# One 128-column part of Strassen's products: a21·d1 + a22·d2 written as (a21 + a22)·d1 + a22·(d2 − d1), in three of four sequence sets and in both down projections

## The chip, the core and the metric

One core of a Trainium2 chip. The time is device microseconds (us) of one execution, the median of several runs. Five engines work side by side, each with its own instruction queue in program order: PE (matmul; PEld is its weight load), DVE (vector), ACT (scalar), POOL (here nearly only a DMA queue that can also add while it writes) and SP (only a DMA queue).

## What is computed

A block of an FNet mixer with a gate: layer norm, a real 2-D Fourier mix by dense matrices, a SwiGLU feed-forward net, and x + mix · silu(ffn). S = 2048, D = 640, F = 1536, all in fp32.

```python
xn = _layernorm(x, axis=-1)
a = jnp.einsum("bsd,ed->bse", xn, dft_hid_re)
b = jnp.einsum("bsd,ed->bse", xn, dft_hid_im)
s = jnp.einsum("ts,bse->bte", dft_seq_re, a) - jnp.einsum("ts,bse->bte", dft_seq_im, b)
g = _silu((_silu(xn @ w_gate) * (xn @ w_up)) @ w_down)
return x + s * g
```

## The kernel before

**The mix** is taken in the other order: first the sequence matrices times xn (function `seq`), then the hidden matrices (`hid`). `seq` runs four times, k = 0 to 3, called sets here: half of the output columns (j = k // 2) with the real or the imaginary matrix (ri = k % 2). Then, for each of the two halves j, `hid(j)`, `gate_up(j)` (12 blocks f of 128 hidden units, gate and up together) and `down(j)` follow one another.

**Strassen.** Each large product is one Strassen step with seven products p1 to p7 instead of eight. The left operand is cut in four: a11, a12, a21, a22 (512 moving columns each; the inner width in chunks g, four of two tiles in `seq`, two of three tiles in `down`). The right operand has 640 columns, which are five blocks of 128: four of them make the 2x2 Strassen step (256 columns each side), and the fifth block is multiplied in the plain way, beside the Strassen products whose left operand is wanted anyway. The fifth block has an upper half d1 and a lower half d2 over the inner width, and two results:

- "d1" (PSUM bank 6) = a11·d1 + a12·d2, which rides on p1 (left a11) and p2 (left a12);
- "d2" (PSUM bank 7) = a21·d1 + a22·d2. Here a22 is p4's left operand, but a21 alone is no product's left operand. So a phase "d" of its own, after p1, splits a21 and multiplies it with d1.

p5's left operand is a21 + a22. In `seq` the sum is made in place by a DMA that adds (`accumulate`, line L589 before, POOL's queue): a21 is loaded (`load`, SP's queue, L576), split for "d", a22 is added to it, and the sum is split for p5. In `down` it is a DVE add into a buffer of its own (L340).

**Split.** fp32 is multiplied as high and low parts: ACT writes the high part (L192), DVE the low part (L197, or L199 with a sign), and each tile pair takes three matmuls (L213 to L215): high·high, high·low, low·high. All split operands lie in one arena, `hl`, all raw data in another, `raw`.

**Order.** Nothing is scheduled by a tool. Class `Plan` records each piece of work with a due time, in units in which one matmul takes MM = 0.226 us; work that feeds a product is due `lead` us ahead of it (`prod`), work that empties a bank after it (`post`). At the end all is sorted by due time and written to the engines' queues in that order; `place` packs all buffers of the whole program into the two arenas by their planned lives and keeps the packing with the lowest penalty for short pauses between two tenants of one place. So a change of any buffer's life can move all other buffers. A tenant that comes too early waits for the last reader of the one before.

For sets 2 to 4 the leads are: loads 17 or 18, the split's high part 10, its low part 8 (`LEAD["S"] = (10, 8)`), right operands 14 for a sum, 13 high, 11 low. The adding DMA of a22 is due 7.5 us ahead of phase "d".

**Down's right operands** (`down_operands`) are split once and kept in DRAM: a generator makes one piece per call (sum or difference on DVE where one is needed, L527; high on ACT, low on DVE, two stores on POOL, L535). `gate_up(0)` calls it twice in each block f from 1 to 10, once after p2 (slot A) and once after the next two products (slot B). Before, 18 pieces fill blocks 1 to 9. `down` fetches them on SP's queue (L996), 14 us ahead of the product for g = 0 and 10 us for g = 1.

**In gate_up** the second bank of each block is used again soon: p7 of block f writes bank b2, DVE empties it (`combine` into `u`, L246), and p4 of the same block writes b2 again after only p1 and p5 of the next block, which are 12 matmuls.

Of the kernel before, what the change touches and what calls it, by code (L numbers as in the profile page):

```python
# [11 lines left out]
ALU = mybir.AluOpType  # L12

P = 128
# [123 lines left out]
def tile_fnet_swiglu(  # L138
# [22 lines left out]
    pl = Plan()  # L161
# [90 lines left out]
    def strassen(tag, groups, get, top, dop, result, end=False):  # L252
# [52 lines left out]
        ops = {}  # L305
# [12 lines left out]
        def phase(p, banks, left, direct=None):  # L318
            w, wk = top(p) if banks else (None, None)
            need(p, left)  # L320
            run(p, ops[p], banks, w, wk, direct)
# [2 lines left out]
            Y[g] = get(11, g)  # L324
            return operand("p1", g, Y[g])

        def a21(g):
            X[g] = get(21, g)
            return operand("d", g, X[g])

        def a12(g):
            Z[g] = get(12, g)
            return operand("p2", g, Z[g])

        def s_1(g):
            V[g] = get(22, g)
            name = pl.buf(("W", tag, g), "raw", n[g])
            W[g] = (name, 0, (name, 0))
            (xn_, xa, xk), (vn, va, vk) = X[g], V[g]
            pl.prod(12, lambda: nc.vector.tensor_tensor(  # L340
                raw(name), raw(xn_, xa, n[g]), raw(vn, va, n[g]), op=ALU.add), [xk, vk], [(name, 0)])
            return operand("p5", g, W[g])
# [13 lines left out]
        phase("p1", b2, a11, (1, 1))  # L356
        s1 = copies("s1")
        evict(s1, b2)
        phase("d", None, a21, (2, 1))
        phase("p2", b1, a12, (1, 2))  # L360
        result(11, b1, s1, ALU.subtract)
        result("d1", (dbank[1],), None, None)
        phase("p5", b3, s_1)
        n5 = copies("n5")
        evict(n5, b3)
        phase("p6", b2, s_2)
# [10 lines left out]
        w, wk = top("p4")  # L377
        need("p4", a22)
        if not end:
            run("p4", ops["p4"], None, None, None, (2, 2))  # L380
            result("d2", (dbank[2],), None, None)
            run("p4", ops["p4"], b2, w, wk)
            result(21, b2, None, None)
            return
        dw, dkeys = dop(2)

        def alone(bank, weights, keys, first, a=0, n=TC):

# [80 lines left out]
    def right(p, g, lead):  # L469


        def quad(h, c, w=256):
            k = 8 * h + 4 * g
            return (lambda a=0, n=4: xn_tiles(k + a, n, 256 * c, w)), [(xn, i, c) for i in range(k, k + 4)]

        def new(what, a, b, op):
            if (what, g) not in sums:
                name = pl.buf((what, g), "raw", 1024)
                view = lambda a=0, n=4: raw(name).rearrange("p (a b) -> p a b", b=256)[:, a:a + n]
                pl.prod(lead, lambda: nc.vector.tensor_tensor(view(), a[0](), b[0](), op=op), [*a[1], *b[1]], [(name, 0)])  # L480
                sums[what, g] = view, [(name, 0)]
            return sums[what, g]

        if p == "p1":
            return quad(0, 0)
        if p == "p2":
            return quad(1, 0)
        if p == "p3":
            return quad(1, 1)
        if p == "p5":  # L490
            return new("nt1", quad(0, 0), quad(0, 1), ALU.subtract)
        if p == "p6":
            return new("t2", quad(1, 1), sums["nt1", g], ALU.add)
        if p == "p4":
            return new("nt4", quad(1, 0), sums["t2", g], ALU.subtract)
        if p == "p7":
            a, b = quad(0, 1), quad(1, 1)
            if ("nt3", g) not in sums:
                pl.prod(lead, lambda: nc.vector.tensor_tensor(a[0](), a[0](), b[0](), op=ALU.subtract), b[1], a[1])
                sums["nt3", g] = a  # L500
            return a
        return quad(int(p[1]) - 1, 2, P)


    d_names = ("p1", "p2", "d1", "d2", "p3", "p5", "p6", "p7", "p4")
    d_dram = {(p, g): dram.tile([P, 768 if p[0] == "d" else 1536], F32, name=f"d_{p}_{g}") for g in range(2) for p in d_names}

    def down_operands():

        for g in range(2):  # L510
            name = pl.buf(("wdn", g), "raw", 6 * D)
            for h in range(2):
                f0 = 6 * h + 3 * g
                pl.prod(8, lambda name=name, f0=f0, h=h: nc.sync.dma_start(
                    raw(name, 3 * h * D, 3 * D).rearrange("p (f d) -> p f d", d=D),
                    wb[f0:f0 + 3, :, 2 * D:].rearrange("f p d -> p f d")), [], [(name, h)])

            def quad(h, c, w=256, name=name):
                return (lambda: raw(name, 3 * h * D, 3 * D).rearrange("p (f d) -> p f d", d=D)[:, :, 256 * c:256 * c + w]), (name, h, c)

            for p in d_names:
                b11, b12, b21, b22 = (quad(*q) for q in ((0, 0), (0, 1), (1, 0), (1, 1)))
                made = {"p5": (b11, b12, ALU.subtract), "p6": (b11, b22, ALU.add),
                        "p7": (b12, b22, ALU.subtract), "p4": (b21, b11, ALU.subtract)}
                if p in made:
                    a, b, op = made[p]
                    pl.prod(1, lambda a=a, b=b, op=op: nc.vector.tensor_tensor(a[0](), a[0](), b[0](), op=op),  # L527
                            [b[1], (name, 0), (name, 1)], [a[1]])
                else:
                    a = {"p1": b11, "p2": b21, "p3": b22, "d1": quad(0, 2, P), "d2": quad(1, 2, P)}[p]  # L530
                n = 768 if p[0] == "p" else 384
                dst = pl.buf(("Tp", p, g), "hl", 2 * n)
                split(0, dst, n, a[0], [a[1], (name, 0), (name, 1)], scale=-1.0 if p == "p1" else None)
                for i in range(2):
                    pl.prod(-4, lambda p=p, g=g, dst=dst, i=i, n=n: nc.gpsimd.dma_start(  # L535
                        d_dram[p, g][:, i * n:i * n + n], hl(dst, i).bitcast(F32)),
                        [(dst, "hl"[i], 0)], [("dd", p, g)], 6)
                yield
# [15 lines left out]
    def seq(k):  # L554
# [157 lines left out]
            return operand("p1", g, Y[g])  # L712

        def p5(g):
            s = operand("p5", g, R[g])
            if fresh:
                accumulate(R[g], 11, g, LEAD["p5", g][1] - 0.1)
            return s

        def d(g):  # L720
            R[g] = load(21, g, 26 if fresh else 18)
            s = operand("d", g, R[g])
            if ("d", g) not in whole:
                accumulate(R[g], 22, g, LEAD["d", g][1] - 0.1 if fresh else 7.5)
            return s

        def p2(g):
# [26 lines left out]
            run(first_two[0])  # L754
        s1 = copy("s1", b2)
        if not fresh:
            run(first_two[1])
        if not fresh:
            product_2()
        run(("p5", p5, b3, None), order=((0, 0), (0, 2), (0, 3), (0, 1)) if fresh else None)  # L760
        n5 = copy("n5", b3)
        if fresh:
            product_2()
# [9 lines left out]
            last.append(operand("p4", g, load(22, g, 17)))  # L773
            return last[-1]

        run(("p4", p4, (), (2, 2)))
        result("d2", (dbank[2],), None, None)
        run(("p4", lambda g: last[g], b2, None))
        result(21, b2, None, None)
# [330 lines left out]
```

## Time and profile before

| what | value |
|---|---|
| median of 3 runs | 994.55 us (992.47 to 995.25) |
| span of the profiled execution | 990.3 us |
| busy share in that span: PE, PEld, DVE, ACT, POOL | 99%, 81%, 72%, 50%, 11% |
| granted PE clock, mean of the span | 1.000 |
| set 1, with the start | to about 113 us |
| sets 2, 3 and 4 | about 113 to 211, to 309, to 407 us |
| gate_up(0), down(0) | about 475 to 622, 622 to 696 us |
| gate_up(1), down(1) | about 764 to 911, 911 to 986 us |

The median stands 4.2 us above the span, since a run also has time ahead of the first and behind the last instruction that the profile shows, and since runs differ. The page's busy numbers are averages over stages with different limits; the waits, told engine by engine, say which engine was ever held up and by whom. The lines themselves stand in the prediction.

### The profile page before, as it was taken

What the parts mean: (1) busy time and instruction counts of PE and PEld (TensorE: products, weight loads), DVE (VectorE), ACT (ScalarE), POOL (GpSimd) and SP (SyncE); (2) the same over time, 40 slices, a digit from 0 to 9 for tenths busy, and PEclk for the clock granted to TensorE, in tenths of its full rate; (3) what the DMA queues carried; (4) which work ended last, traced back from release to release, by engine and by line L of the source; (5) the groups of instructions that cost most, each with busy time, mean ns of one, the idle gap of its engine ahead of it and who ended that gap; (6) DMA issues with size and microseconds to landing.
All of it is one profiled execution on the core that took longest, in us unless ns stands there. A gap on an engine that the chain in (4) does not pass through costs nothing. (4 is left out here: it accounts for less than half of the span.)

```text
span 990.3 us, 11726 instructions
## 1 busy us (share of the span) xinstructions
PE 981.1 (99%) x4302; PEld 802.9 (81%) x4302; DVE 710.3 (72%) x927; ACT 497.2 (50%) x712; POOL 105.0 (11%) x175
## 2 busy tenths in 40 slices
PE   8999999999999999999999999999999999999998
PEld 4778888888888888888888888888888888887887
DVE  6999667856785686377678787777577566666686
ACT  5775554655465564434555654444334544445342
POOL 1640201010101010000111110000010100000000
PEclk9999999999999999999999999999999999999999
DMA  9995757675766586832447535679951301106673
GB/s 342 242 226 168 249 136 179 208 210 116 189 219 187 117 236 205 275 135 94 160 149 263 189 139 176 214 258 335 332 177 54 107 28 53 54 27 205 227 266 131
DMA packets 71464, 180.08 MB, mean 182 GB/s; under 512 B 6448, under 2 KB 22064, under 8 KB 71408
## 3 DMA queue, kind: packets, MB, share of 16 engines
q1 hardware_dynamic: 57072, 125.71, 38.0%
q0 software_dynamic: 14336, 53.63, 19.7%
q8 instruction: 33, 0.54, 0.2%
q14 instruction: 23, 0.19, 0.1%
HBM read 145.75 MB, written 33.57 MB: 181 GB/s over the span
## 5 line engine op out<-in xcount | busy, mean ns | idle before, releaser
L213 PE MATMUL ps<-hl 128*128 128x512 f32 x1420 | 551.9, 389 | 1.3 <-ACT raw L979 0.7
L215 PE MATMUL ps<-hl 128*128 128x512 f32 x1420 | 551.5, 388 | 1.1 <-DVE hl L197 1.0
L214 PE MATMUL ps<-hl 128*128 128x512 f32 x1420 | 551.4, 388 | 0.3 <-DVE hl L197 0.3
L192 ACT ACTIVATE hl<-raw 128x1024 fp32r<-128x1024 f32 (+6 forms) x503 | 371.9, 788 | 263.5 <-PE ps L214 63.1
L197 DVE TENSOR_TENSOR hl<-raw,hl 128x1024 fp32r<-128x1024 f32 (+5 forms) x432 | 391.2, 936 | 133.1 <-ACT hl L192 68.3
L213 PEld LDWEIGHTS ps<-hl 128*128 128x128 f32 x1420 | 266.6, 188 | 59.6 <-ACT hl L192 3.2
L215 PEld LDWEIGHTS ps<-hl 128*128 128x128 f32 x1420 | 266.6, 188 | 57.7 <-DVE hl L197 1.8
L214 PEld LDWEIGHTS ps<-hl 128*128 128x128 f32 x1420 | 266.6, 188 | 55.3 <-DVE hl L197 0.8
L241 ACT ACTIVATE raw<-ps 128x512 f32<-128x512 f32 (+1 forms) x122 | 80.3, 676 | 128.9 <-PE ps L215 111.7
L246 DVE TENSOR_TENSOR raw<-ps,raw 128x512 f32<-128x512 f32 (+1 forms) x90 | 71.5, 795 | 58.8 <-PE ps L215 57.7
L980 DVE TENSOR_TENSOR raw<-raw 128x512 f32<-128x512 f32 x24 | 16.6, 692 | 49.3 <-ACT raw L979 49.2
L893 DVE TENSOR_TENSOR raw<-raw 128x256 f32<-128x256 f32 (+1 forms) x96 | 47.7, 518 | 0.0
L199 DVE SCALAR_TENSOR_TENSOR hl<-raw,hl 128x384 fp32r<-128x384 f32 (+5 forms) x71 | 43.0, 605 | 4.9 <-PE ps L214 2.5
L589 POOL DMA_DIRECT2D raw<-in_cs x36 | 31.8, 953 | 132.4 <-DVE raw L592 88.4
L592 DVE TENSOR_TENSOR raw<-raw 128x1024 f32<-128x1024 f32 x28 | 34.1, 1217 | 8.7 <-DMA raw<-in_cs 8.7
L1042 POOL DMA_DIRECT2D out<-raw x10 | 6.7, 672 | 303.1 <-ACT hl L192 187.5
L693 POOL DMA_DIRECT2D p_dram<-raw x24 | 17.2, 758 | 201.8 <-DVE raw L246 151.8
L958 ACT ACTIVATE raw<-raw 128x512 f32<-128x512 f32 x24 | 15.2, 632 | 22.8 <-DVE raw L246 22.8
L846 DVE TENSOR_TENSOR raw<-raw 128x1024 f32<-128x1024 f32 (+1 forms) x24 | 23.9, 1040 | 1.7 <-DMA raw<-in_xt 1.7
L818 POOL DMA_DIRECT2D y_dram<-raw x20 | 10.9, 546 | 132.5 <-ACT raw L241 132.5
L979 ACT ACTIVATE raw<-ps 128x512 f32<-128x512 f32 x24 | 14.3, 595 | 19.2 <-PE ps L215 17.4
L535 POOL DMA_DIRECT2D d_p<-hl x28 | 15.1, 541 | 80.9 <-ACT hl L192 66.9
(48 smaller groups left out, 196.5 us busy)
## 6 DMA issues: line engine op xcount, KB each, us to landing
raw<-in_cs SPq DMA_DIRECT2D x79, 512.0 KB, 6.3
hl<-d_p SPq DMA_DIRECT2D x56, 384.0 KB, 4.3
raw<-in_cs POOLq DMA_DIRECT2D x36, 512.0 KB, 8.4
raw<-in_wb SPq DMA_DIRECT2D x24, 640.0 KB, 3.9
d_p<-hl POOLq DMA_DIRECT2D x28, 384.0 KB, 3.0
raw<-p_dram SPq DMA_DIRECT2D x8, 1280.0 KB, 9.3
p_dram<-raw POOLq DMA_DIRECT2D x16, 512.0 KB, 5.7
raw<-in_hd SPq DMA_DIRECT2D x20, 320.0 KB, 8.4
```

The lines of the kernel that those rows point to most:

```text
L192: nc.scalar.activation(like(hl(dst, 0, a, n)), src(), AF.Copy, scale=1.0 if scale is None else scale)
L197: nc.vector.tensor_tensor(lo, src(), hi, op=ALU.subtract)
L199: nc.vector.scalar_tensor_tensor(lo, src(), scale, hi, op0=ALU.mult, op1=ALU.subtract)
L213: nc.tensor.matmul(o, w(0), m(0), start=first, stop=False, skip_group_check=True)
L214: nc.tensor.matmul(o, w(0), m(1), start=False, stop=False, skip_group_check=True)
L215: nc.tensor.matmul(o, w(1), m(0), start=False, stop=True, skip_group_check=True)
L241: pl.post(lambda: nc.scalar.activation(wide(raw(dst, a, n)), pair(b), AF.Copy), pkeys(b), [(dst, a)], after)
L246: pl.post(lambda: nc.vector.tensor_tensor(wide(raw(dst, a, n)), pair(b), wide(raw(other)), op=op), [*pkeys(b), (other, 0)], [(dst, a)], after)
L589: pl.prod(lead, lambda: nc.gpsimd.dma_start(wide(raw(name)), source(q, g), accum_op=ALU.add), [], [(name, 0), (name, 1)], 8)
L592: pl.prod(lead, lambda: nc.vector.tensor_tensor(raw(dst), raw(dst), raw(src), op=ALU.add), [(src, 0)], [(dst, 0)])
L846: pl.prod(46 - 6 * q - 2 * i - half, lambda i=i, op=op, part=part, rows=rows, nb=nb: nc.vector.tensor_tensor(part(), part(), raw(rows, i * ...
L893: pl.prod(lead, lambda o=o, a=a, b=b, op=op: nc.vector.tensor_tensor(o(), a(), b(), op=op), [(w, 0)], [(c, lead)])
```

## The change

In sets 2 to 4 and in both `down` calls the result "d2" is now computed as (a21 + a22)·d1 + a22·(d2 − d1). The first product rides on p5, whose left operand is that sum, the second on p4. Phase "d" and its split of a21 go away there. A third right operand "d3" = d2 − d1 is new: in `seq` a DVE difference `nt5` (made once, kept to the end of set 4) and a split in each of the three sets; in `down` one more piece per g from the generator, which now makes 20 pieces and fills blocks 1 to 10. Set 1 keeps the old way. In sets 2 to 4 the load of a21 is now due 26 us and the adding DMA of a22 18 us ahead of p5.

```diff
@@ strassen (down)
-        def a21(g):
-            X[g] = get(21, g)
-            return operand("d", g, X[g])
...
         def s_1(g):
-            V[g] = get(22, g)
+            X[g], V[g] = get(21, g), get(22, g)
...
-        phase("d", None, a21, (2, 1))
         phase("p2", b1, a12, (1, 2))
...
-        phase("p5", b3, s_1)
+        phase("p5", b3, s_1, (2, 1))
...
-            run("p4", ops["p4"], None, None, None, (2, 2))
+            run("p4", ops["p4"], None, None, None, (2, 3))
...
-        dw, dkeys = dop(2)
+        dw, dkeys = dop(3)
@@ right (seq)
+        if p == "d3":
+            return new("nt5", quad(1, 2, P), quad(0, 2, P), ALU.subtract, P)
@@ down_operands
-    d_names = ("p1", "p2", "d1", "d2", "p3", "p5", "p6", "p7", "p4")
+    d_names = ("p1", "p2", "d1", "d2", "d3", "p3", "p5", "p6", "p7", "p4")
...
+                        "d3": (quad(1, 2, P), quad(0, 2, P), ALU.subtract)}
@@ seq
         def p5(g):
+            if not fresh:
+                R[g] = load(21, g, 26)
+                accumulate(R[g], 22, g, 18)
             s = operand("p5", g, R[g])
...
         if not fresh:
-            run(first_two[1])
-        if not fresh:
             product_2()
-        run(("p5", p5, b3, None), order=((0, 0), (0, 2), (0, 3), (0, 1)) if fresh else None)
+        run(("p5", p5, b3, None if fresh else (2, 1)), order=((0, 0), (0, 2), (0, 3), (0, 1)) if fresh else None)
...
-        run(("p4", p4, (), (2, 2)))
+        run(("p4", p4, (), (2, 2 if fresh else 3)))
```

How the instructions now stand. PE's list has the same 4309 rows in the same order with the same shapes; only which operands they read and which bank they write differs. DVE, all forms counted: 12 low splits of 128x1024 and 4 of 128x1536 go; 6 of 128x512, 2 of 128x384, 2 differences of 128x512 and 2 of 128x384 come. ACT: 12 high splits of 128x1024 and 4 of 128x1536 go, 6 of 128x512 and 2 of 128x384 come. POOL has 4 more stores, SP 8 more fetches.

POOL's queue in set 2 (`raw<-in_cs` is an adding DMA, `p_dram<-raw` a store of a result). Before:

```order
54 L693 DMA p_dram_74<-raw_66 128x2x512
55 L589 DMA raw_66<-in_cs 128x1024 x7
56 L693 DMA p_dram_74<-raw_66 128x2x512
57 L693 DMA p_dram_74<-raw_66 128x512
58 L589 DMA raw_66<-in_cs 128x1024
```

And now:

```order
54 L691 DMA p_dram_74<-raw_66 128x2x512
55 L587 DMA raw_66<-in_cs 128x1024 x5
56 L691 DMA p_dram_74<-raw_66 128x2x512
57 L691 DMA p_dram_74<-raw_66 128x512
58 L587 DMA raw_66<-in_cs 128x1024 x3
```

The first four of the eight adding DMAs feed p5, in both versions ahead of everything else in this stretch; the two stores of p2's results now stand ahead of three of the four that feed p7.

DVE in gate_up(0), block 10 (`L527`, now `L525`, is a generator's difference, `L246` empties a bank, `hl<-raw,hl` is a low split). Before, with no piece in this block:

```order
438 L197 TENSOR_TENSOR hl<-raw,hl 128x384
439 L246 TENSOR_TENSOR raw<-ps,raw 128x512
440 L197 TENSOR_TENSOR hl<-raw,hl 128x256
441 L199 SCALAR_TENSOR_TENSOR hl<-raw,hl 128x384
442 L246 TENSOR_TENSOR raw<-ps,raw 128x512
443 L966 TENSOR_TENSOR raw<-raw 128x512
444 L893 TENSOR_TENSOR raw<-raw 128x256
445 L246 TENSOR_TENSOR raw<-ps,raw 128x512
446 L197 TENSOR_TENSOR hl<-raw,hl 128x384
```

And now, with pieces p7 and p4 of g = 1:

```order
456 L197 TENSOR_TENSOR hl<-raw,hl 128x384
457 L525 TENSOR_TENSOR raw<-raw 128x3x256
458 L246 TENSOR_TENSOR raw<-ps,raw 128x512
459 L197 TENSOR_TENSOR hl<-raw,hl 128x256
460 L199 SCALAR_TENSOR_TENSOR hl<-raw,hl 128x384
461 L197 TENSOR_TENSOR hl<-raw,hl 128x768
462 L246 TENSOR_TENSOR raw<-ps,raw 128x512
463 L965 TENSOR_TENSOR raw<-raw 128x512
464 L525 TENSOR_TENSOR raw<-raw 128x3x256
465 L892 TENSOR_TENSOR raw<-raw 128x256
466 L246 TENSOR_TENSOR raw<-ps,raw 128x512
467 L197 TENSOR_TENSOR hl<-raw,hl 128x384
468 L197 TENSOR_TENSOR hl<-raw,hl 128x768
```

The last L246 in each of the two lists is the one that p4 waits for; one more difference now stands right ahead of it. Blocks whose two slots both hold a piece with such a 768-wide difference were 4, 8 and 9; now they are 4, 5, 9 and 10.

SP's fetches for down(0)'s p4, as they now stand (before, only the rows of d_p4 were there):

```order
48 L995 DMA hl_65<-d_p4_0_84 128x768 x2
49 L995 DMA hl_65<-d_d3_0_79 128x384 x2
50 L995 DMA hl_65<-d_p4_1_94 128x768 x2
51 L995 DMA hl_65<-d_d3_1_89 128x384 x2
```

They stand ahead of the loads for the last results of that product.

`place` also gives nearly all buffers other places, from the first set on. From its table of places and due times: before, no split part in gate_up(0) came onto a buffer whose last reader was a store to DRAM due less than 6 us earlier. Now six do:

| split part (engine) | due | comes onto, whose store is due |
|---|---|---|
| p2, g 0, low (DVE) | 485.0 | p1, g 0, low, 482.9 |
| p3, g 0, high (ACT) | 507.4 | d3, g 0, high, 507.3 |
| p4, g 0, low (DVE) | 533.8 | p7, g 0, high, 531.7 |
| p2, g 1, low (DVE) | 546.0 | p1, g 1, low, 543.9 |
| p6, g 1, low (DVE) | 582.6 | p5, g 1, high, 580.5 |
| down(0)'s p1, g 0, high (ACT) | 598.0 | p4, g 1, high, 596.8 |

More of the change, by code (lines that the diff above doesn't have):

```diff
@@ L474, in quad, with new @@
             return (lambda a=0, n=4: xn_tiles(k + a, n, 256 * c, w)), [(xn, i, c) for i in range(k, k + 4)]
-        def new(what, a, b, op):
+        def new(what, a, b, op, w=256):
             if (what, g) not in sums:
-                name = pl.buf((what, g), "raw", 1024)
-                view = lambda a=0, n=4: raw(name).rearrange("p (a b) -> p a b", b=256)[:, a:a + n]
+                name = pl.buf((what, g), "raw", 4 * w)
+                view = lambda a=0, n=4: raw(name).rearrange("p (a b) -> p a b", b=w)[:, a:a + n]
                 pl.prod(lead, lambda: nc.vector.tensor_tensor(view(), a[0](), b[0](), op=op), [*a[1], *b[1]], [(name, 0)])
@@ L523, in down_operands @@
                 made = {"p5": (b11, b12, ALU.subtract), "p6": (b11, b22, ALU.add),
-                        "p7": (b12, b22, ALU.subtract), "p4": (b21, b11, ALU.subtract)}
+                        "p7": (b12, b22, ALU.subtract), "p4": (b21, b11, ALU.subtract),
+                        "d3": (quad(1, 2, P), quad(0, 2, P), ALU.subtract)}
                 if p in made:
@@ L720, in d @@
         def d(g):
-            R[g] = load(21, g, 26 if fresh else 18)
+            R[g] = load(21, g, 26)
             s = operand("d", g, R[g])
             if ("d", g) not in whole:
-                accumulate(R[g], 22, g, LEAD["d", g][1] - 0.1 if fresh else 7.5)
+                accumulate(R[g], 22, g, LEAD["d", g][1] - 0.1)
             return s
```

## The prediction

> **What bounds the kernel now.** I read the page's first part, then the busy time by stretches, then the waits of PE and PEld alone, then the groups with their shapes.
>
> ```profile
> PE 981.1 (99%) x4302; PEld 802.9 (81%) x4302; DVE 710.3 (72%) x927; ACT 497.2 (50%) x712; POOL 105.0 (11%) x175
> PEclk9999999999999999999999999999999999999999
> ```
>
> PE is busy for 99% of the span at the full granted clock. A busy PE need not be a PE at its peak, so the pace has to be checked. The stretches (start:end, length, then each engine's busy us and instructions, granted clock, DMA share, GB/s):
>
> ```profile
> 100.00:900.00 800.00, 799.94 (x3529) 661.87 (x3528) 562.45 (x739) 396.10 (x595) 71.37 (x111) 1.00 0.54 171
> 900.00:985.00 85.00, 84.31 (x385) 70.06 (x384) 59.46 (x47) 34.56 (x32) 2.72 (x4) 1.00 0.64 222
> 113.30:211.20 97.90, 97.90 (x433) 81.09 (x433) 68.44 (x61) 52.36 (x56) 11.01 (x14) 1.00 0.67 189
> 622.50:696.00 73.50, 73.50 (x326) 60.83 (x326) 56.38 (x44) 31.58 (x29) 3.28 (x5) 1.00 0.82 273
> ```
>
> In 800 us PE ran 3529 matmuls, one each 800/3529 = 0.2267 us. Set 2 (third row) has 7 products x 8 tiles x 2 banks x 3 matmuls and 4 x 8 x 3 for the fifth block, 432 in all: 432 x 0.2267 = 97.9 us, its whole length. So PE runs at one pace without a gap, whatever operand it reads. Who ever held it up after set 1's start, in the waits of 62 to 985 us (us in total, times, longest):
>
> ```profile
> PEld ps L213 <- ACT raw L979: 1.1, 1, 1.1
> PEld ps L213 <- DVE raw L246: 0.9, 3, 0.5
> PE ps L213 <- ACT raw L979: 0.7, 1, 0.7
> ```
>
> The first and the third are one event, down(1)'s start behind the last silu that empties a bank; the second are three short waits in gate_up(0). That is 2.0 us in 923. Anything that merely frees DVE or ACT elsewhere can give back no more than that.
>
> **The change part by part.** *PE.* Its list has the same rows before and now: the 24 matmuls of phase "d" in each set, and the 18 in each `down`, ride on p5 instead. At one pace for all operands this costs and saves 0.0 us. *DVE and ACT*, by their groups (busy us, mean ns of one):
>
> ```profile
> L197 DVE TENSOR_TENSOR hl<-raw,hl 128x1024 fp32r<-128x1024 f32 x185 | 218.8, 1219 | 68.2 <-ACT hl L192 29.1 <-issue 21.2 <-PE ps L215 10.7
> L192 ACT ACTIVATE hl<-raw 128x1024 fp32r<-128x1024 f32 x191 | 191.6, 1051 | 107.5 <-PE ps L215 30.5 <-PE ps L214 25.9 <-DVE raw L860 14.5
> L197 DVE TENSOR_TENSOR hl<-raw,hl 128x1536 fp32r<-128x1536 f32 x32 | 55.7, 1754 | 13.9 <-ACT hl L192 8.4 <-PE ps L215 3.4 <-PE ps L214 1.4
> L192 ACT ACTIVATE hl<-raw 128x1536 fp32r<-128x1536 f32 x32 | 46.8, 1484 | 35.9 <-DVE raw L290 15.8 <-PE ps L214 14.6 <-PE ps L215 5.2
> L197 DVE TENSOR_TENSOR hl<-raw,hl 128x512 fp32r<-128x512 f32 x60 | 41.1, 686 | 26.7 <-issue 8.2 <-ACT hl L192 7.7 <-PE ps L214 6.3
> L192 ACT ACTIVATE hl<-raw 128x384 fp32r<-128x384 f32 x76 | 38.4, 513 | 0.0
> L192 ACT ACTIVATE hl<-raw 128x512 fp32r<-128x512 f32 x61 | 37.6, 625 | 27.4 <-PE ps L215 17.4 <-PE ps L214 7.9 <-DVE raw L846 2.1
> L197 DVE TENSOR_TENSOR hl<-raw,hl 128x384 fp32r<-128x384 f32 x52 | 28.5, 551 | 0.8 <-ACT hl L192 0.6 <-PE ps L215 0.2
> L980 DVE TENSOR_TENSOR raw<-raw 128x512 f32<-128x512 f32 x24 | 16.6, 692 | 49.3 <-ACT raw L979 49.2
> ```
>
> DVE loses 12 x 1.219 + 4 x 1.754 = 21.6 us and gets 6 x 0.686 + 2 x 0.692 + 2 x 0.551 and two 384-wide differences at about the same 0.551, 7.7 us: 13.9 us less. ACT loses 12 x 1.051 + 4 x 1.484 = 18.6 and gets 6 x 0.625 + 2 x 0.513 = 4.8: 13.8 us less. In sets and `down` neither was waited for, so this saves 0.0 us of the span. What hides the added work: `nt5` and d3's split are due 14, 13 and 11 us ahead of p4, beside p7 (48 x 0.2267 = 10.9 us); without that cover it would be 0.69 + 0.63 + 0.69 = 2.0 us at the start of each set's p4. The d3 fetches in `down` have 10 to 14 us.
>
> *p5's operand in sets 2 to 4.* The adding DMA had the whole of p2 as cover; now it has 18 us, and the split waits for it. The adding line and the load it adds to (duration min/median/max in ns; landing in us):
>
> ```profile
> L589 POOL DMA_DIRECT2D raw<-in_cs x36: 851/871/1874, 21.6 to 353.4; - x36
> DMA to landing us min/median/max: 5.3/8.4/16.4
> DMA to landing us min/median/max: 3.1/6.3/12.1
> ```
>
> The second row is of the adds, the third of SP's loads (L576). A load has 26 − 18 = 8 us, 6.3 at the median. The add lands at 8.4, then 1.05 on ACT and 1.22 on DVE: 18 − 8.4 − 2.3 = 7.3 us to spare. At the longest landing, 18 − 16.4 − 2.3 = −0.7: PE would wait 0.7 us once a set, 2.1 us in all. Queued behind a waiting split on ACT is the copy of p1's banks, and p6, which writes these next, comes only after p2 and p5. The 16.4 us stand in set 1, where four adds are issued together; here they come one per chunk, 18 matmuls or 4.1 us apart. I take 0.0, bounds 0.0 and +2.1. The Trainium skill, "SBUF — State Buffer" (section "SBUF: two separate sides"), says that DVE in a two-port mode can keep POOL from writing a DMA's descriptors, and gives about 620 ns alone against 3100 overlapped. Here the longest issue is 1.0 us above the median, and 2.5 us more would still leave 4.8 of the 7.3, so the sum by that rule is the same, but it makes the upper end likelier.
>
> *gate_up(0).* This is where PE does wait. The timeline of block 9's end:
>
> ```profile
> 597.12 0.95 DVE L527 TENSOR_TENSOR raw<-raw 128x768 f32<-128x768 f32 x1
> 597.99 0.42 DVE L893 TENSOR_TENSOR raw<-raw 128x256 f32<-128x256 f32 x1
> 598.11 1.15 ACT L192 ACTIVATE hl<-raw 128x768 fp32r<-128x768 f32 x2 [2.81 <-DVE raw L527]
> 598.33 0.68 DVE L246 TENSOR_TENSOR raw<-ps,raw 128x512 f32<-128x512 f32 x1
> 599.06 0.19 PEld L213 LDWEIGHTS ps<-hl 128*128 128x128 f32 x1 [0.48 <-DVE raw L246]
> ```
>
> Slot B's difference, 0.95 us, runs ahead of the L246 that empties p4's bank, and PE waits 0.48 us. The three waits of 0.9 us match the three blocks with a difference in both slots (4, 8, 9): 0.48 in block 9, which follows another such block, and 0.4 for the other two, 0.2 each. Now there are four such blocks, in two runs of two: 2 x (0.2 + 0.5) = 1.4 us, so **+0.5 us**. Bounds: −0.9 (all gone) and four times 0.5 less 0.9, +1.1.
>
> *The six new buffer waits.* A generator's store:
>
> ```profile
> DMA to landing us min/median/max: 2.1/3.0/7.1
> ```
>
> With 3.0 us to land, the four on DVE with 2.1 us between the due times wait 0.9 each, the two on ACT 2.9 and 1.8: 8.3 us at most if PE got all of it. I take 0.0: on DVE the low part stands behind the L246 that PE waits for (order lists), and delays only weights of the next block. On ACT the wait takes the place of one that is there: the 2.81 us in the row above is ACT idle in slot B for the difference, and the new tenant p3 needs none.
>
> **The sum**: 990.3 + 0.0 (PE) + 0.0 (DVE, ACT relief) + 0.0 (adds) + 0.5 (gate_up) + 0.0 (buffers) = 990.8 us of span. The runs' median is 994.55 − 990.3 = 4.2 us above the span, so 995.0 us.
>
> **The rivals.** A measurement of this kernel tells about 0.3%, 3 us, from no change: faster is under 991.6, slower over 997.5.
>
> *Buffer waits reach PE (slower).* Place: gate_up(0), which has the highest DVE load of the long stages beside its bank hand-offs:
>
> ```profile
> 475.00:622.50 147.50, 147.44 (x650) 121.49 (x649) 112.25 (x208) 82.49 (x162) 22.16 (x41) 1.00 0.53 186
> ```
>
> 112 of 147.5 us, 76%. If the four DVE waits are passed on, 3.6 us: 994.55 + 3.6 = 998.2; with the two on ACT 1002.9. It decides from a landing of 2.9 us on, if nothing hides it. For it: stores landed as late as 7.1. Against it: the order and the 24% of DVE left. A stall costs its own length as long as the clock holds, as after the 1.1 us wait at down(1)'s start (granted 1.00 in 900 to 985). The Trainium skill, "TensorE: Matmul & The Clock Gate" (section "Part 1: The HAM clock gate"), puts the half-rate state after an idle window of about 3.4 us; a wait of that length, which no row after 62 us shows, would cost more by it.
>
> *The add lands late (slower).* 2.1 us at the longest landing seen, 996.7; from 16.7 us on, or if POOL comes to its issue 1.0 us late on top (3 x 1.7 = 5.1 us, 999.7), it is slower.
>
> *The relief ends the waits.* All 2.0 us go: 992.6. Against it: down(1)'s wait is for a silu that the change leaves where it is.
>
> *Set 1 gets better places (faster).* Its instructions are unchanged, its buffers move, and it is the one stage where PE waits for splits, in 9 to 65 us:
>
> ```profile
> PEld ps L213 <- ACT hl L192: 3.2, 4, 1.3
> PEld ps L215 <- DVE hl L197: 1.8, 2, 0.9
> PEld ps L215 <- DVE hl L199: 0.9, 3, 0.6
> PEld ps L214 <- DVE hl L197: 0.8, 1, 0.8
> ```
>
> 6.7 us; half of it gives 991.2. Against it: ACT's own idle time there is for DMAs and DVE, not for PE to leave a buffer.
>
> *It does not do what it says.* The words could mean a product less; PE's equal lists exclude it.
>
> **How the numbers follow.** Forecast 995.0: 0.60. Buffer waits: 0.12, slower. Late adds: 0.10, half within 0.3%, half slower. Relief: 0.08, within. Set 1: 0.10, faster. So faster 0.10, within 0.3% 0.60 + 0.05 + 0.08 = 0.73, slower 0.12 + 0.05 = 0.17. The range goes from 992.0 (the lowest run before, 992.47, and the relief's 992.6) to 998.5 (the DVE waits' 998.2). The likeliest case alone is 993.0 to 996.5, about the spread of the runs before.
>
> **What would show it.** Right: PE again one matmul each 0.2267 us from 100 to 900, no PE wait behind an adding DMA, four instead of three waits of PEld for the line that empties banks (L246), 1.4 us in all; DVE near 696 and ACT near 483 us busy. Wrong: a PE wait for L192 or L197 at p5 of sets 2 to 4 (late adds); waits for L192 in 500 to 625 us (buffers); a first 62 us that is shorter or longer by over 1 us; or a pace of PE other than 0.2267, which would upset the ground of the whole sum.

## The result, and the profile after

| | before | after |
|---|---|---|
| median of 18 runs each, on the same chip | 992.57 us (990.85 to 995.52) | 998.53 us (995.10 to 1001.18) |
| ratio of the runs, 95% interval | | 1.0054 [1.0044, 1.0065] |
| span of the profiled execution | 990.3 us | 998.5 us |
| mean granted PE clock of that span | 1.000 | 0.996 |

The change makes the kernel slower by about 5.4 us (0.0054 x 992.57; the two medians lie 6.0 us apart). The forecast was 995.0 us, no change; its range ended at 998.5, and the median stands at that end. The rival "buffer waits reach PE" is what happened, mainly at another of its six places than those its first price was for.

First the page of the kernel after: busy time, and the granted clock.

```profile
PE 985.3 (99%) x4302; PEld 804.2 (81%) x4302; DVE 694.8 (70%) x923; ACT 482.5 (48%) x704; POOL 107.4 (11%) x179
...
PEclk9999999999999999999999999999999999999999
```

DVE has 15.5 us less work than before and ACT 14.7 less; POOL has 2.4 more. PE's busy time, with the same instructions, is 4.2 us longer. At slices of 25 us the clock row shows nothing. The groups of the splits (busy us, mean ns of one) are as costed, 12 of each kind fewer at an unchanged price:

```profile
L197 DVE TENSOR_TENSOR hl<-raw,hl 128x1024 fp32r<-128x1024 f32 x173 | 205.1, 1219 | 74.6 <-ACT hl L192 55.1 <-PE ps L215 9.6 <-PE ps L214 5.1
L192 ACT ACTIVATE hl<-raw 128x1024 fp32r<-128x1024 f32 x179 | 180.3, 1052 | 96.3 <-DVE raw L590 28.4 <-DMA raw<-in_cs 19.5 <-PE ps L214 15.4
```

Who held up PE, then PEld, from 62 to 985 us (us in total, times, longest):

```profile
PE ps L213 <- ACT raw L241: 3.9, 2, 3.5
PE ps L213 <- ACT raw L978: 0.7, 1, 0.7
PE ps L213 <- DVE raw L246: 0.2, 1, 0.2
...
PEld ps L213 <- ACT raw L241: 4.8, 2, 3.9
PEld ps L213 <- DVE raw L246: 1.7, 4, 0.6
PEld ps L213 <- ACT raw L978: 1.1, 1, 1.1
PEld ps L214 <- DVE hl L197: 0.5, 1, 0.5
```

New is L241, the copy on ACT of a bank. It made PE wait 3.5 us at one time (the other time, 0.5 us, is in set 3). The stretches (start:end, length, each engine's busy us and instructions, granted clock, DMA share, GB/s), first two of those that were shown of before, then the 22 us around that wait:

```profile
113.30:211.20 97.90, 97.90 (x434) 81.06 (x433) 66.06 (x61) 49.71 (x54) 11.13 (x14) 1.00 0.63 177
...
475.00:622.50 147.50, 143.72 (x629) 117.55 (x629) 112.84 (x213) 81.98 (x164) 24.31 (x45) 1.00 0.48 171
...
612.00:618.00 6.00, 5.91 (x26) 4.59 (x25) 4.01 (x8) 3.07 (x6) 1.08 (x2) 1.00 0.89 261
618.00:622.00 4.00, 0.64 (x3) 0.19 (x1) 0.39 (x1) 1.91 (x2) 0.00 (x0) 0.91 1.01 401
622.00:628.00 6.00, 5.88 (x14) 4.63 (x15) 3.54 (x4) 2.17 (x3) 0.00 (x0) 0.50 1.02 390
628.00:634.00 6.00, 6.00 (x28) 4.94 (x27) 3.48 (x5) 2.62 (x3) 0.00 (x0) 0.99 0.32 94
```

Set 2 takes the same 97.9 us. In gate_up(0), PE stands still for nearly 4 us from 618, and then works for 6 us at a granted clock of 0.50: it counts as busy, with 14 matmuls where 26 are usual. By these rows the clock is at 0.50 for 6.8 us in all, from about 621.3 to 628.1 us: 0.7 us of that lie in the row of 0.91, and 0.1 in the row of 0.99. Now the place itself: ACT's timeline (start, length, then what it waited for before), the PE's, and the one store on POOL that was issued at 613.1 us.

```profile
615.77 0.52 ACT L192 ACTIVATE hl<-raw 128x384 fp32r<-128x384 f32 x1
620.09 1.48 ACT L192 ACTIVATE hl<-raw 128x1536 fp32r<-128x1536 f32 x1 [3.81 <-DMA d_p<-hl]
621.48 0.58 ACT L241 ACTIVATE raw<-ps 128x512 f32<-128x512 f32 x1
```

```profile
618.25 0.39 PE L215 MATMUL ps<-hl 128*128 128x512 f32 x1
622.12 0.80 PE L213 MATMUL ps<-hl 128*128 128x512 f32 x1 [3.48 <-ACT raw L241]
622.71 0.63 PE L214 MATMUL ps<-hl 128*128 128x512 f32 x1
623.13 0.63 PE L215 MATMUL ps<-hl 128*128 128x512 f32 x1
...
627.83 0.52 PE L214 MATMUL ps<-hl 128*128 128x512 f32 x1
628.19 0.40 PE L215 MATMUL ps<-hl 128*128 128x512 f32 x1
```

```profile
L533 POOL DMA_DIRECT2D d_p<-hl x1: 540/540/540, 613.1 to 613.1; - x1
...
who waited for it (us, times):
  ACT hl L192: 3.8, 1
...
DMA to landing us min/median/max: 6.9/6.9/6.9
```

The store is the generator's last but one, p4 g 1 high. It took 6.9 us to land. Its buffer's next tenant is the high part of down(0)'s p1 g 0 (plan: due 598.0, which the profile's clock reaches some 18 us later), a split for the next stage, not urgent. But ACT works in order: it stood idle 3.81 us for that buffer, made the 1.48 us split, and only then the copy L241 of `u2`, which empties the bank that p7 of block 11, the last block, writes. From 618.25 to 622.12 is 3.87 us between two matmuls, 3.64 more than one pace. The 14 matmuls from 622.12 to 628.19 take 6.07 us instead of 3.17, another 2.90.

One more of the six new waits shows in this trace, the first of the table of due times: DVE's low split of p2 g 0, behind the store of p1 g 0 low that was issued at 498.4 us and took 5.9 us to land.

```profile
504.38 0.96 DVE L197 TENSOR_TENSOR hl<-raw,hl 128x768 fp32r<-128x768 f32 x1 [3.55 <-issue]
```

DVE stood idle 3.55 us. PE noticed little of it: DVE then worked with only two short pauses (0.63 and 0.32 us) up to an L246 that ended at 514.08, and the matmul that needed that bank came 0.46 us late. In copy_first and filler, described below, DVE waits 3.1 and 3.2 us here and PEld 0.2 at that bank; in holdlast8 neither waits.

**The whole difference of the two spans**, by when the same matmul starts in both traces: start and set 1 −0.35 us, set 3's p3 +1.18, the gate waits of gate_up(0) ahead of block 11, less those of before, +0.48 (0.46 of it the one at 514 us), block 11 +6.88 (3.64 + 2.90, and one gate wait of 0.36), and from there to the end 0.0; sum +8.2 = 998.5 − 990.3. Set 3's part is a load that waits for the buffer of a stored "d1" result and lands late; the traces of the other kernels with these sets show 0 to 0.4 us there.

The runs' 5.4 us are less than this pair's 8.2. Of the 18 runs after, 14 have a mean clock of 0.996 to 0.998 and 4 one of 1.000, so the half pace seems not to come every time; and set 1 varies on its own, which the last experiment takes up.

### The profile page after: what moved, and what is told of

It reads as the page before. It is cut to its first block, busy times and chain, and to the rows that moved or that the text cites. A ratio compares the mean times of both kernels' runs of the same rounds, so it can differ in the third digit from the quotient of the medians.

```text
span 998.5 us, 11703 instructions
## 1 busy us (share of the span) xinstructions
PE 985.3 (99%) x4302; PEld 804.2 (81%) x4302; DVE 694.8 (70%) x923; ACT 482.5 (48%) x704; POOL 107.4 (11%) x179
## 4 chain that ended last, share of the span: by engine, by line
PE 87%; DMA 5%; DVE 2%; issue 2%; ACT 2%; POOL 1%; SPq 0%; DVEq 0%; POOLq 0%; ACTq 0%
PE ps L213 29%; PE ps L215 29%; PE ps L214 29%; DMA raw<-in_cs 2%; DMA raw<-in_x 2%; DVE hl L197 1%; ACT hl L192 1%; DMA p_dram<-raw 1%; DMA d_p<-hl 1%; ACT raw L451 0%; DVE raw L590 0%; ACT raw L241 0%; POOL d_p L533 0%; DVE raw L246 0%; DVE raw L475 0%
## 5 line engine op out<-in xcount | busy, mean ns | idle before, releaser
L192 ACT ACTIVATE hl<-raw 128x1024 fp32r<-128x1024 f32 (+6 forms) x495 | 358.0, 773 | 230.6 <-DVE raw L892 54.6
L197 DVE TENSOR_TENSOR hl<-raw,hl 128x1024 fp32r<-128x1024 f32 (+5 forms) x424 | 374.7, 915 | 131.1 <-ACT hl L192 99.8
L241 ACT ACTIVATE raw<-ps 128x512 f32<-128x512 f32 (+1 forms) x122 | 80.1, 675 | 171.2 <-PE ps L215 146.5
L246 DVE TENSOR_TENSOR raw<-ps,raw 128x512 f32<-128x512 f32 (+1 forms) x90 | 71.5, 795 | 71.0 <-PE ps L215 70.5
L1036 ACT ACTIVATE raw<-raw 128x1024 f32<-128x1024 f32 x6 | 6.4, 1062 | 38.6 <-DVE raw L246 32.8
```

The source lines that it names most:

```text
L192: nc.scalar.activation(like(hl(dst, 0, a, n)), src(), AF.Copy, scale=1.0 if scale is None else scale)
L197: nc.vector.tensor_tensor(lo, src(), hi, op=ALU.subtract)
L241: pl.post(lambda: nc.scalar.activation(wide(raw(dst, a, n)), pair(b), AF.Copy), pkeys(b), [(dst, a)], after)
L246: pl.post(lambda: nc.vector.tensor_tensor(wide(raw(dst, a, n)), pair(b), wide(raw(other)), op=op), [*pkeys(b), (other, 0)], [(dst, a)], after)
```

## The experiments

Theory A: the store's landing behind one ACT wait, and the half pace after it, are nearly the whole loss; the arithmetic costs nothing. The rivals: the traffic and operands of the new arithmetic cost it; or any stall costs only its own length. Each ratio is to runs of before taken in the same rounds on the same chip, so it is not always the quotient of two medians shown here. Since set 1 varies between executions, the last column gives, from the traces, the time from one matmul behind set 1's p2 (at about 77 us) to the same one in down(0) (at about 653 us), less that of before, 576.27 us.

| kernel | median us | ratio to before, 95% | behind set 1, us |
|---|---|---|---|
| after | 998.53 | 1.0054 [1.0044, 1.0065] | +8.5 |
| copy_first | 995.05 | 1.0018 [1.0002, 1.0033] | +2.5 |
| holdlast8 | 992.97 | 0.9999 [0.9986, 1.0012] | +0.2 |
| filler | 997.43 | 1.0032 [1.0017, 1.0046] | +4.6 |
| bef_shift | 1001.53 | 1.0079 [1.0056, 1.0102] | +8.2 |
| seq_only | 992.62 | 1.0007 [0.9993, 1.0020] | +0.3 |
| down_only | 1000.55 | 1.0085 [1.0065, 1.0105] | +7.1 |
| alternate | 994.13 | 0.9999 [0.9982, 1.0016] | −0.5 |
| bef_alt | 993.79 | 0.9995 [0.9979, 1.0010] | −0.5 |
| alt_ln | 992.56 | 1.0005 [0.9995, 1.0014] | −0.5 |
| bef_ln | 993.39 | 1.0008 [0.9998, 1.0018] | 0.0 |

**copy_first: the copy goes ahead of the waiting split.** Buffers unchanged; only the place of one instruction in ACT's list.

```diff
     where.update(pl.place({"hl": HL_KB * 256, "raw": RAW_KB * 256}))
+    names = [o[3] for o in pl.ops]
+    late = next(i for i, n in enumerate(names) if (("S", ("down", 0), "p1", 0), "h") in n)
+    copy = next(i for i, n in enumerate(names) if ("u2", 0, NF - 1) in n)
...
+    pl.ops.insert(copy, pl.ops.pop(late))
```

> The changed kernel with two neighbours on ACT's list exchanged: in block 11 of gate_up(0) the copy of p6's bank (u2) now stands ahead of down(0)'s first split, which waits for a store to land on its buffer. All buffers keep their places, so the wait itself stays. Theory A (the time is lost because the bank copy stands behind that waiting split, so that PE waits 3.9 us in block 11 and then runs about 6 us at half pace): the wait of PE for L241 and the 427 ns matmuls vanish, a wait of at most 1 us appears at down(0)'s p1; of the 8.2 us between the two profiles 1.3 + 0 to 1 us remain; ratio to before 0.999 to 1.003. Rival B (the time is lost to the late adds at p5, to more traffic or to the layout as a whole): ratio stays at 1.005.

No wait for L241 is left and no matmul at half pace. ACT still waits for the store, and passes a part on. Who held up PE there, and DVE's rows:

```profile
PE ps L213 <- DVE raw L246: 1.4, 1, 1.4
```

```profile
619.85 1.76 DVE L197 TENSOR_TENSOR hl<-raw,hl 128x1536 fp32r<-128x1536 f32 x1 [4.07 <-ACT hl L192]
621.53 1.28 DVE L246 TENSOR_TENSOR raw<-ps,raw 128x512 f32<-128x512 f32 x2
```

Behind its gate wait, block 11 loses 1.75 us instead of 6.54 (3.64 + 2.90). The order on ACT is thus the way from the store to PE; swapping it takes away the long wait and the half pace. What stays goes the same way on another queue: the low part of the late split waits for ACT on DVE, and the L246 that empties a bank stands behind it. That wait of 1.4 us was expected at down(0)'s p1 and at 1 us at most.

**holdlast8: that one store's buffer is kept longer.** `place` is told that the store of p4 g 1 needs 8 us instead of 6, so that it deals other tenants; by its table none of the six pairs is left.

```diff
-                        [(dst, "hl"[i], 0)], [("dd", p, g)], 6)
+                        [(dst, "hl"[i], 0)], [("dd", p, g)], 8 if (p, g) == ("p4", 1) else 6)
```

> The changed kernel with one planner number changed: the two stores of the last right-operand piece (p4, g = 1) are taken to hold their buffer 8 us instead of 6. The planner then gives other places, and by its table no split part of gate_up(0) or of down(0)'s start comes onto a buffer whose store is due less than 6 us earlier; all seven or so instructions per piece are the same. Theory A: PE's wait for L241 in block 11 and the half pace are gone, the waits for L246 in blocks 4, 5, 9 and 10 stay (about 1.4 us), the wait of set 3's p3 stays (about 1 us): ratio 0.999 to 1.003. Rival B (the arithmetic of the change costs the time): 1.005.

The loss is gone: 0.9999, +0.2 us behind set 1. The stores landed no sooner. Line L533 in 594 to 640 us, and the gate waits:

```profile
DMA to landing us min/median/max: 2.6/2.7/7.4
```

```profile
PEld ps L213 <- DVE raw L246: 1.3, 4, 0.5
```

A store of 7.4 us costs nothing where nobody needs its buffer. The four gate waits that the forecast counted, behind blocks 4, 5, 9 and 10, are all there; set 3's wait, which was expected to stay, is not. Since this kernel removes all six pairs, it is copy_first that tells which one cost the most.

**filler: PE kept busy through the wait.** 18 bf16 matmuls into a bank that is free, ahead of block 11's p7; the wait stays. They are work that the kernel before and after does not have.

```diff
+                if j == 0 and f == NF - 1 and p == "p7":
+                    pl.post(lambda: busy(ps[:, 0], 18), [], [("ps", 0)])
                 product(todo, reads)
```

> The changed kernel with 18 bf16 matmuls into the unused bank 0 ahead of block 11's p7 in gate_up(0), where PE stood still for 3.9 us; they take 18 x 0.213 = 3.8 us at full pace, so they fill the wait and compute nothing that is used. If the half pace after the wait comes from PE having stood still: PE runs 0.227 us a matmul behind them and about 2.9 us of the 8.2 are won back, ratio about 1.002 to 1.003 against 1.005. If the slow matmuls have another cause (operands arriving late, a bank in use): they stay, ratio 1.005 or more.

Granted clock in the stretches before, in and after the wait:

```profile
618.00:622.00 4.00, 3.93 (x19) 2.31 (x18) 1.03 (x2) 1.97 (x2) 0.00 (x0) 1.00 1.01 356
622.00:626.00 4.00, 4.00 (x19) 2.76 (x18) 1.74 (x2) 1.56 (x2) 0.00 (x0) 1.00 1.03 401
```

The clock is 1.00 throughout, and the matmuls behind the wait run at full pace while the DMA engines are as busy (1.03) as in the kernel after (1.02). What is saved behind set 1 is 8.5 − 4.6 = 3.9 us: the half pace (2.9) and most of set 3's 1.2. One thing weakens this trace: its set 1 was late, so PE reached the place at 619.60 us and not at 618.25, while the copy came at about the same time. Without the 18 matmuls PE would have stood still for only some 2.3 us (an estimate from these times), and no trace here shows half pace after so short a wait. The runs speak more clearly: all nine have a mean clock of 0.999 or 1.000, against 0.996 to 0.998 in 14 of the 18 of the kernel after. So the 2.9 us go with PE's standing still, and not with the traffic; the next experiment shows half pace at little traffic.

**bef_shift: the same conflict in the kernel before.** Old arithmetic; the generator starts one block later, so that it ends in block 10. The line stands twice, for slots A and B.

```diff
-            if j == 0 and f and f != NF - 1:
+            if j == 0 and f > 1 and f != NF - 1:
                 next(spare, None)
```

> The kernel before, with its arithmetic, but the generator of right operands begun one block later, so that its 18 pieces fill blocks 2 to 10 instead of 1 to 9. No instruction is added or taken away. By the planner's table down(0)'s first split (ACT, due 598.0) then comes onto the buffer of the last piece, whose store is due at 596.8, as in the changed kernel. Theory A: PE waits 3 to 4 us for L241 in block 11 and then runs at half pace, 4 to 7 us, ratio 1.004 to 1.007. Rival B (the change's arithmetic, adds or fetches cost the time): ratio 1.000.

PE's wait in 500 to 640 us, and the clock behind it:

```profile
PE ps L213 <- ACT raw L241: 5.7, 1, 5.7
```

```profile
624.00:630.00 6.00, 4.55 (x11) 3.59 (x12) 2.60 (x3) 3.40 (x4) 0.00 (x0) 0.50 0.11 18
```

The loss of the change, +8.2 us behind set 1, without one instruction of the change; in other parts, though: 5.8 us of standing still and 2.3 at half pace. The wait and the ratio (1.0079) are above what was expected (3 to 4 us, 1.004 to 1.007). The DMA engines were busy for 0.11 of the time in this row, so traffic is not what slows these matmuls.

**seq_only and down_only: each half of the change alone.** seq_only keeps `strassen` and `down_operands` as before; down_only keeps `right` and `seq` as before. Against the kernel after, the lines that matter:

```diff
@@ seq_only
-    d_names = ("p1", "p2", "d1", "d2", "d3", "p3", "p5", "p6", "p7", "p4")
+    d_names = ("p1", "p2", "d1", "d2", "p3", "p5", "p6", "p7", "p4")
@@ down_only
-        if p == "d3":
-            return new("nt5", quad(1, 2, P), quad(0, 2, P), ALU.subtract, P)
...
-            if not fresh:
-                R[g] = load(21, g, 26)
-                accumulate(R[g], 22, g, 18)
```

> The change in sets 2 to 4 alone; both `down` and the generator's list of pieces are as before. Theory A (the store of p4 g 1 high meets its buffer's next tenant at 598.0 and holds the u2 copy that p7 of block 11 waits for; nothing else costs more than 1 or 2 us): the list has no piece d3, the buffers are dealt as before and the conflict is not there, so no PE wait for L241 and no matmuls at 427 ns; three gate waits for L246, 0.9 us; what may stay is set 3's wait of 1.2 us; ratio to before 0.999 to 1.002. Rival B (the arithmetic itself costs: the p5 sum over the inner width, its adding DMA and the longer p5 operand in the sets): about two thirds of the loss is here, ratio 1.003 to 1.004, with PE waits for L192 or L197 at p5 of sets 2 to 4.

> The change in both `down` alone, with d3 in the generator's list; the sets are as before. Theory A: the list of pieces is that of the changed kernel, p4 g 1 high falls on the buffer that down(0)'s p1 g 0 high is due on at 598.0, so a PE wait for L241 of 3 to 6 us in block 11 and some 12 matmuls at 427 ns behind it come back; set 3's wait does not; ratio 1.003 to 1.007. Rival B: two of six differences' worth of the loss at most, in the two `down` themselves and not in gate_up(0); ratio 1.000 to 1.002.

seq_only, PEld from 62 to 985 us:

```profile
PEld ps L213 <- DVE raw L246: 1.1, 3, 0.5
PEld ps L213 <- ACT raw L982: 1.1, 1, 1.1
```

down_only, PE in 500 to 640 us, and the two stores of p4 g 1 (line L531):

```profile
PE ps L213 <- ACT raw L241: 3.9, 1, 3.9
```

```profile
DMA to landing us min/median/max: 7.2/7.3/7.4
```

Three sets of new arithmetic cost nothing: from matmul to matmul, sets 2 to 4 together take 0.05 us more than before, and 0.2 us lie in gate_up(0). All of the loss comes with the generator's longer list. In the runs down_only loses more than the whole change (1.0085 against 1.0054, over the 1.007 expected), in its trace less (+7.1 against +8.5, of which 1.2 are set 3's); this difference was not followed up.

**alternate and bef_alt: the list in another order.** The kernel after, and the kernel before, with pieces that have a difference and pieces that have none taking turns.

```diff
@@ alternate
-    d_names = ("p1", "p2", "d1", "d2", "d3", "p3", "p5", "p6", "p7", "p4")
+    d_names = ("p1", "p5", "p2", "p6", "d1", "p7", "d2", "p4", "p3", "d3")
@@ bef_alt
-    d_names = ("p1", "p2", "d1", "d2", "p3", "p5", "p6", "p7", "p4")
+    d_names = ("p1", "p5", "p2", "p6", "d1", "p7", "d2", "p4", "p3")
```

> The changed kernel with one line of it in another order: the generator's list of pieces alternates those with a difference and those without (p1 p5 p2 p6 d1 p7 d2 p4 p3 d3). Theory A: no new tenant falls due within the 3 us of a store's landing, so no wait for L241 in block 11 and no half pace (6.9 us less than the changed kernel's profile); no block has a 768-wide difference in both slots, so the four gate waits for L246 (1.7 us in the changed kernel, 0.9 before) go too; set 3's wait of 1.2 us may stay. Ratio to before 0.998 to 1.001. Rival B: the work is that of the changed kernel to the last instruction, so the ratio stays at 1.004 to 1.006.

> The kernel before with the list of its nine pieces alternated in the same way (p1 p5 p2 p6 d1 p7 d2 p4 p3), the arithmetic untouched. It asks whether the alternating order is worth something by itself. Theory A: the three gate waits of 0.9 us go, no buffer conflict comes, ratio 0.998 to 1.000, and between this kernel and the changed kernel with the alternated list there is at most set 3's 1.2 us, 0.001. Rival B: as before, 1.000, and the changed kernel with the alternated list stands 0.004 to 0.006 above it.

alternate, PEld from 62 to 985 us:

```profile
PEld ps L213 <- ACT hl L192: 1.2, 1, 1.2
PEld ps L213 <- ACT raw L978: 1.1, 1, 1.1
PEld ps L215 <- DVE hl L197: 0.9, 1, 0.9
```

No wait for L246 or L241 is left; the first and third rows are the end of a late set 1. Both kernels take the same 575.73 us behind set 1. The change as arithmetic is therefore worth 0.0 us, and between the two orders of the list lie 9.1 us in the traces of the new kernel (1.2 of them in set 3, where no other trace shows more than 0.4), 0.5 in those of the old.

**alt_ln and bef_ln: why runs of one kernel differ by 3 us.** The 18 runs of before fall into ten from 990.85 to 992.58 us and eight from 994.55 to 995.52, with none between. In the first ten traces the same matmul behind set 1's p2 starts at 75.4 to 77.3 us in five and at 79.4 to 80.0 in the other five. POOL's small layer norm operations for the third pair of chunks, and the DVE row beside them: first copy_first (early), then holdlast8 (late).

```profile
49.37 3.28 DVE L197 TENSOR_TENSOR hl<-raw,hl 128x1024 fp32r<-128x1024 f32 x4
...
48.67 0.19 POOL L441 TENSOR_SCALAR sm<-mv 128x2 f32<-128x2 f32 x1
...
49.39 1.24 POOL L444 TENSOR_SCALAR sm<-sm 128x2 f32<-128x2 f32 x1
...
51.31 0.26 POOL L446 TENSOR_TENSOR sm<-sm,rowst 128x2 f32<-128x2 f32 x1
```

```profile
49.59 3.25 DVE L197 TENSOR_TENSOR hl<-raw,hl 128x1024 fp32r<-128x1024 f32 x4
...
49.67 1.15 POOL L441 TENSOR_SCALAR sm<-mv 128x2 f32<-128x2 f32 x1
...
51.84 1.05 POOL L444 TENSOR_SCALAR sm<-sm 128x2 f32<-128x2 f32 x1
52.98 1.05 POOL L445 TENSOR_TENSOR rowst<-sm 128x2 f32<-128x2 f32 x1
54.11 0.20 POOL L446 TENSOR_TENSOR sm<-sm,rowst 128x2 f32<-128x2 f32 x1
```

An operation of 0.2 us on POOL takes over 1 us while DVE runs L197. The late execution starts the chain 1 us later, so more of it falls beside the four L197, and it ends 2.7 us later. Both kernels move that pair's chain to DVE:

```diff
-                layer_norm(8 + 2 * g, 2, *LEAD["xn", 4 + g], nc.gpsimd)
+                layer_norm(8 + 2 * g, 2, *LEAD["xn", 4 + g], nc.vector if g == 2 else nc.gpsimd)
```

> The changed kernel with the alternated list, and besides in set 1 the eight small layer norm operations of the third pair of chunks moved from POOL to DVE (five there and one on ACT, as the first four pairs have them). In the ten profiles so far set 1 ended either early or about 2.7 us later, with the same instructions; the late ones have that pair's last POOL operation end at 54.0 to 54.7 us of the span instead of 50.1 to 52.0, each of its operations 1.0 to 1.25 us instead of 0.2 while DVE runs L197 of 128x1024. Theory S (the two clusters of runs, near 992 and 995 us, are these two ways of set 1): the runs fall into one cluster, the lower one, near 990 us, and the ratio to before is 0.996 to 0.998. Rival T (the clusters come from something else, the late small operations are only a sign of it): two clusters stay 2.5 to 3 us apart, ratio 0.999 to 1.001. Should DVE be the tighter engine there, its five operations and the wait for ACT's square root put 1 to 2 us on every run: one cluster, ratio 0.998 to 1.001.

> The kernel before with the same move of the third pair's small operations to DVE. Theory S: one cluster of runs near 991 us, ratio 0.997 to 0.999; and the kernel with the alternated list and the same move stands 0.5 to 1 us below it, the three gate waits. Rival T: two clusters as before, ratio 1.000.

(The times in these two expectations are counted from 0.25 us later than the profile's clock.) The gap between the clusters closes: 12 runs of alt_ln from 991.65 to 994.32, 12 of bef_ln from 991.62 to 994.33, filled between. But the middle stays, ratios 1.0005 and 1.0008: the third case of the expectation, one cluster near 992.5 to 993.4 and no gain. For bef_ln this is a miss: 0.997 to 0.999 was expected. The medians of the two lie 0.8 us apart, as expected (0.5 to 1), but their intervals overlap. That set 1's chain made the clusters is supported by this; what DVE pays for the move was not taken apart. No kernel of this study is measurably faster than before.

## Where the prediction was right and where wrong, point by point

The likeliest case, no change, did not come. That the measured median still stands at the end of the range is luck on two counts: the base of 994.55 us came from three runs, and 18 runs gave 992.57; and the end of the range, 998.5, was taken from waits on DVE that were not the cause.

- **One pace for all operands, 0.0 us: right.** Set 2 takes 97.90 us as before, and seq_only's sets agree to 0.05 us. The sign that was given, this pace from 100 to 900 us, fails only in block 11 and, for 1.2 us, at set 3's p3.
- **DVE and ACT, 13.9 and 13.8 us less in the splits, DVE near 696 and ACT near 483 busy: right** (694.8 and 482.5, so 15.5 and 14.7 us less; in ACT's sum 18.6 should be 18.5), and worth 0.0 us, as said.
- **p5's operand and the late adds: right to take 0.0.** No wait of PE at p5 of sets 2 to 4 appears; that rival is out.
- **gate_up(0), +0.5 us: right in mechanism, the size near.** In the kernel after there are four waits of PEld behind L246, 1.7 us instead of the 1.4 foreseen, and they cost PE 0.48 + 0.36 = 0.84 us more than those of before (ahead of block 11, and in it). But one of the four, at 514 us, 0.46 us, comes from a buffer wait; that leaves 0.4. In holdlast8, where no pair is left, all four stand where they were foreseen, 1.3 us.
- **The six new buffer waits, 0.0: this is the step that failed**, for one of the six. The sentence was "On ACT the wait takes the place of one that is there". It holds for p3 g 0 high, due 507.4: at its place, 524.2 us in the trace, ACT was idle for 2.10 us and PE was not held up. The row with 2.81 us of idle ACT was from another place, block 9. For down(0)'s p1 g 0 high, due 598.0, nothing was read at its place: there the copy of `u2` stands behind the split on ACT, and p7 of block 11 needs it; the rule to name what is queued behind a waiting instruction was kept for DVE and not for this one. The split of p2 g 0 low on DVE waited too, 3.55 us, and there the order hid it but for 0.46 us. The second error was the landing, 3.0 us from the median, where this store meets the fetches for down(0) (DMA share 0.89 in 612 to 618 us) and takes 6.9.
- **The price of a stall.** The rival's first price let it cost its own length; it cost 3.64 us, and 2.90 more at half pace. The forecast's sentence on a longer stall names the reason. The rival's 998.2 is near the measured 998.53 for another sum: it had four DVE waits of 0.9 us that PE pays in full. One of these was 3.55 us and PE paid 0.46; none of the others held up PE. Its sign, waits for L192 in 500 to 625 us, did not appear on PE either: PE waited for the copy L241, and ACT for the landing ahead of L192.
- **"It decides from a landing of 2.9 us on"** was wrong as a condition: the store of p1 g 0 low took 5.9 us to land and cost PE 0.46, and holdlast8 had a landing of 7.4 us and no loss. It takes a late landing, a tenant due within it, and work behind that tenant in the same queue that PE needs.

What stays open: why 4 of the 18 runs have a mean clock of 1.000 (their waits were not profiled; these four ran from 995.10 to 998.71 us), and how much of the 6.9 us is due to the fetches; no kernel moved these apart.

## What to carry to other kernels

When a change adds a buffer or lengthens a list, look at every new pair of tenants whose first one ends in a store, and for each ask what is queued behind the waiting instruction and who needs that; here a wait of 3.55 us on DVE cost PE 0.46, and one of 3.81 on ACT cost it 6.54, more than everything else together. Price a wait of nearly 4 us, the shortest here that brought it, with the half pace behind it: all three such waits that were traced had the clock at 0.50 for 6.8 us. And test a change apart from the places it happens to move things to: here a reordered list of ten names undid the whole loss, and the same disturbance in the old kernel brought it back.

## What the hardware showed that was not expected

- **Half pace after one wait.** Gaps of 3.9, 4.3 and 6.1 us between two matmuls (after, down_only, bef_shift) were followed by 6.1, 6.1 and 4.8 us with matmuls 427 ns apart instead of 227, at a granted clock of 0.50. In all three this clock lasted 6.8 us, from 3.0, 3.4 and 4.0 us after the start of the last matmul on; so in these three the part of the 6.8 us that fell into the wait cost nothing more, and the longest wait had the shortest slow stretch behind it. Gaps of 1.8 us (copy_first) and 1.1 us (down(1)'s start) were followed by none, nor was the wait filled with 18 other matmuls. The Trainium skill, "TensorE: Matmul & The Clock Gate" (section "Part 1: The HAM clock gate"), says half rate after an idle window of about 3.4 us; the 3.0 to 4.0 us of these traces lie around it.
- **A store's landing is no constant.** In the kernel after, half of the generator's stores took 2.1 to 2.8 us. The two issued in 612 to 615 us took 6.9 and 7.5 us, and two issued in 538 to 541 us 7.0 and 7.4; the 16 DMA engines were 0.89 to 1.01 busy in 612 to 622 us, and 0.97 in 538 to 548 us.
- **Small POOL operations beside DVE.** 128x2 operations took 0.19 to 0.20 us alone; beside L197 of 128x1024 (1.22 us each) most of those shown took 1.05 to 1.24 us, and some others 0.26 to 0.64. The Trainium skill, "SBUF — State Buffer" (section "Who interferes with whom"), says that a DVE instruction with two inputs in SBUF contends with a GpSimd instruction that reads SBUF, and that the loser waits for the whole of it; the rows agree.
